# Modulation as matrix products with one moving column, D transform's matrices in eight loads, and a new order in the first stage

## The chip, the cores and the metric

One core of a Trainium2 chip runs the kernel. The metric is the device time of one execution in microseconds. Engines are named as in the profile: PE is TensorE, DVE is VectorE, ACT is ScalarE, POOL is GpSimd, SP is SyncE (which here only issues DMA transfers). Clocks are shares of full speed.

## The reference

`S` is 2048 rows, `D` is 512 columns, `F` is 1792. All data are float32.

```python
mod = (_silu(c) @ w_mod).reshape(c.shape[0], 6, 1, -1)
sa, ca, ga, sb, cb, gb = (mod[:, 0], mod[:, 1], mod[:, 2], mod[:, 3], mod[:, 4], mod[:, 5])
h = _layernorm(x, axis=-1) * (1 + ca) + sa
a = einsum("bsd,ed->bse", h, dft_hid_re)
b = einsum("bsd,ed->bse", h, dft_hid_im)
x = x + ga * (einsum("ts,bse->bte", dft_seq_re, a) - einsum("ts,bse->bte", dft_seq_im, b))
h = _layernorm(x, axis=-1) * (1 + cb) + sb
x = x + gb * ((_silu(h @ w1) * (h @ w3)) @ w2)
```

## The kernel before

The kernel has three stages. The first is the transform along D: eight steps `k`, each of two blocks of 128 rows (a block and its mirror), are loaded, normalised, turned by TensorE, modulated with `sa` and `1 + ca`, split into a high part (float32r, by ScalarE) and a low part (by VectorE), and multiplied with the D transform's matrices. The second stage is the transform along S, the third the gated feed-forward block. Stage two begins with the products at L750.

What the first stage needs ahead of any product is loaded in this order, mostly from SP's queue: the condition `cc`, the first rows `x` (k = 0), four tiles `wm[v, k]` of the modulation's weights (`v` 1 is the scale `ca`, 0 is the shift `sa`; two tiles from ACT's queue, the fourth tile in two loads), the D transform's matrices for two of four column groups `dt` (`raw_w[0]`, `raw_w[1]`: real and imaginary part, 512 KB a tile), the rows of k = 1, the matrices' other two tiles, and the rows of k = 2 and 3. A load's completion is counted on one of eight semaphores in turn, and a load waits for the one eight before it.

A matrix tile has its 128 partitions as two halves `q` of 64: partition 64 q + r holds the source's row (r, q), and in the source q lies inside r. Before, each half of each part is a load of its own, whose source has 64 rows: `queue.dma_start(raw_w[dt][q * 64 : (q + 1) * 64, m, :], w[i][par::2, q])`, 16 loads in all (L231). ScalarE (`w_highs`) and VectorE (`w_lows`, `differ_w`) then make the operands `wu`, `wn` and `wd` of them.

The modulation before: `mod_scale` multiplies the four quarters of a weight matrix by `silu(c)` and adds them up, one ScalarE and three VectorE instructions for each `v`; `mod_sum` sums over the partitions with four 128-column products with ones; `mod_read` copies the sums to `mod1`.

`keep_warm` is a product on data of no use, which keeps TensorE busy while it has nothing to do.

The work of the first stage is put in order by a list scheduler written in the kernel (`task` and `arrange`): each task has a rank (a number from the table `RANK`, plus the step `k` times `PACE`), needs, and a planned duration on an engine; among the tasks that could begin soon the one with the lowest rank is taken. `at` gives the planned times at which loads land and the modulation is there, `clear` the planned times at which the engines are free. These numbers set the order alone; on the chip every engine takes its instructions in that order and waits by semaphores. Where TensorE would stand idle in the plan, while the first products are not there, `arrange` puts in small filler products.

Of the kernel before, what the change touches and what calls it, by code (L numbers as in the profile page):

```python
# [12 lines left out]
OP = mybir.AluOpType  # L13
AX = mybir.AxisListType

P = 128
# [6 lines left out]
ND = D // P  # L23
# [19 lines left out]
def folded(nc, pools, c, cp, wmr, wmc, x, xt, ctr, cti, wdr, wdi, w1, w3, w2, out):  # L43
# [15 lines left out]
    def take(dt=F32, what="s"):  # L59
        slot = free.popleft()  # L60
        count[0] += 1
        t = big.tile([P, 2, N], dt, name=f"{what}_{count[0]}", tag=f"slot{slot}")
        slot_of[id(t)] = (slot, t)
        return t

    def give(t):
        slot, _ = slot_of.pop(id(t))
        free.append(slot)

    def bank(i):  # L70
        count[0] += 1
        return psum.tile([P, N], F32, name=f"bank{i}_{count[0]}", tag=f"bank{i}")

    def flat(t):
        return t.rearrange("p a b -> p (a b)")
# [7 lines left out]
    def cols(i):  # L83
        return slice(i * P, (i + 1) * P)

    def copy(dst, src, scale=1.0):
        nc.scalar.activation(dst, src, AF.Copy, scale=scale)  # L87
# [62 lines left out]
    mirror = consts.tile([P, NT, 2, NK // 2], I32, name="mirror")  # L150
# [64 lines left out]
    wm = {}  # L215
# [8 lines left out]
    raw_w = {}  # L224

    def load_hid(dt, queue):
        i, par = HD[dt]
        raw_w[dt] = take(F32, "w")
        for m, w in enumerate((wdr, wdi)):
            for q in range(2):  # L230
                queue.dma_start(raw_w[dt][q * 64 : (q + 1) * 64, m, :], w[i][par::2, q])  # L231

    nc.sync.dma_start(cc, cp)
    load_x(0, nc.scalar)
# [4 lines left out]
    for dt in range(2):  # L239
        load_hid(dt, nc.sync)  # L240
    load_x(1)
    for dt in range(2, ND):
        load_hid(dt, nc.sync)
# [27 lines left out]
    zero = take(F32, "zero")  # L271
    nc.gpsimd.memset(flat(zero), 0.0)
    first_tmp = take(F32, "tmp")
    onesf = first_tmp[:, 0, :]
# [3 lines left out]
    def keep_warm(count, width=N):  # L278

        for _ in range(count):  # L280
            nc.tensor.matmul(
                warm[:, :width], onesf[:, :P], onesf[:, :width], start=True, stop=True
            )

    sc = consts.tile([P, ND], F32, name="sc")
# [8 lines left out]
    def hid_cols(t, dt):  # L294

        i, par = HD[dt]
        return t[:, 2 * P * i + par : 2 * P * (i + 1) : 2]

    mod_acc = [bank(5), bank(6)]

    def mod_scale(v, h):

        w, own = wm[v, 0][:, 0, :], wm[v, h]
        if h == 0:
            copy_by(w, w, sc[:, 0:1])
        for n in range(1 - h, 2):
            nc.vector.scalar_tensor_tensor(
                w, own[:, n, :], sc[:, 2 * h + n : 2 * h + n + 1], w, op0=OP.mult, op1=OP.add
            )

    def mod_sum(v):

        for dt in range(ND):
            nc.tensor.matmul(
                mod_acc[v][:, cols(dt)],
                hid_cols(wm[v, 0][:, 0, :], dt),
                onesf[:, :P],
                start=True,
                stop=True,
            )  # L320

    def mod_read(v):
        for at in (slice(0, ND),) if v else [slice(dt, dt + 1) for dt in range(ND)]:
            nc.vector.tensor_scalar(
                mod1[:, v, at],
                mod_acc[v][:, ::P][:, at],
                float(v),
                None,
                op0=OP.add,
            )  # L330
        for h in range(2):
            give(wm.pop((v, h)))

    def copy_by(dst, src, by):
        nc.scalar.activation(dst, src, AF.Identity, scale=by)  # L335
# [116 lines left out]
    def norm_root(k):  # L452
        mv, r = rs[k]
        nc.scalar.activation(r[:, 0, :], mv[:, :, 1], AF.Sqrt, bias=eps, scale=1.0)

    def norm_inverse(k):

        mv, r = rs[k]
        nc.vector.reciprocal(r[:, 0, :], r[:, 0, :])
        nc.vector.scalar_tensor_tensor(  # L460
            r[:, 1, :], mv[:, :, 0], -1.0, r[:, 0, :], op0=OP.mult, op1=OP.mult
        )

    def norm_scale(k, side, engine):
        r = rs[k][1]
        a, by, add = xz[k][:, side, :], r[:, 0, side : side + 1], r[:, 1, side : side + 1]
        if engine == "ACT":
            nc.scalar.activation(a, a, AF.Identity, bias=add, scale=by)
        else:
            nc.vector.tensor_scalar(a, a, by, add, op0=OP.mult, op1=OP.add)  # L470


    turned, hm, hs, h1 = {}, {}, {}, {}
    hh, hl = {}, {}
# [5 lines left out]
    def turn_rows(k, side):  # L480
        if side == 0:
            turned[k] = [bank(2 * (k % 2) + h) for h in range(2)]
        for dt in range(ND):
            at = (dt % 2) * HALF + side * P
            nc.tensor.transpose(
                turned[k][dt // 2][:, at : at + P],
                hid_cols(xz[k][:, side, :], dt),
                anti if side and where(k)[1] else ident,
            )
        if side:  # L490
            give(xz.pop(k))
            rs.pop(k)

    def modulate_rows(k, dt, engine):
        if k not in hm:
            hm[k] = take(F32, "hm")
        src = turned[k][dt // 2][:, (dt % 2) * HALF : (dt % 2 + 1) * HALF]
        dst = four(hm[k])[:, dt, :]
        sa, ca1 = mod1[:, 0, dt : dt + 1], mod1[:, 1, dt : dt + 1]
        if engine == "ACT":  # L500
            nc.scalar.activation(dst, src, AF.Identity, bias=sa, scale=ca1)
        else:
            nc.vector.tensor_scalar(dst, src, ca1, sa, op0=OP.mult, op1=OP.add)
# [35 lines left out]
    uh, us, ul = {}, {}, {}  # L539
# [6 lines left out]
    def hid_begin(k):  # L546

        hb[k] = bank(4 + k % 2)
        nc.tensor.matmul(
            hb[k], nought, flat(wt[0] if k else zz)[:, :N], start=True, stop=False, skip_group_check=True  # L550
        )
# [102 lines left out]
    def clear_z():  # L654
        copy(flat(zz), flat(zero))
        give(zero)
# [139 lines left out]
    xr = {}  # L796

    def load_xt(t):
        xr[t] = [take(F32, "xr") for _ in range(2)]
        for i in range(2):  # L800
            nc.sync.dma_start(xr[t][i], xt[t, i])

    def residual(t, e, src, gate):
        xs = xr[t][e // 2][:, e % 2, :]
# [261 lines left out]
    turn = [0, 0]  # L1066
# [360 lines left out]
    clear = {"PE": 0.0, "DVE": 0.0, "ACT": 0.0, "POOL": 0.0, "SP": 0.0}  # L1427
# [32 lines left out]
    def at(us, *names):  # L1460
        for name in names:
            ends[name] = (us, "DMA")

    def last_steps(k):
# [6 lines left out]

    PACE = 7.39
    RANK = {
        "stats": -18.2,
        "root": -47.5,
        "inverse": -47.1,
        "scale": -41.6,
        "turn": -4.3,
        "mod": -3.8,
        "sum": -42.2,  # L1480
        "hh": -19.0,
        "hl": -6.5,
        "h1": -11.0,
        "prod": 2.1,
        "odd": -9.0,
        "mirror": 61.7,
        "uh": 12.4,
        "us": 4.0,
        "ul": 3.9,
        "diff": 21.3,  # L1490
        "up": -6.8,
        "ush": 27.9,
        "ulh": 31.5,
    }
    seq_steps = []
    keep_warm(3)
# [1 line left out]
        norm_stats(0, side)  # L1498
    norm_root(0)
    norm_inverse(0)  # L1500
    for side in range(2):
        norm_scale(0, side, "ACT" if side else "DVE")
        turn_rows(0, side)
    keep_warm(1)
    for v, h in ((1, 0), (1, 1), (0, 0)):
        mod_scale(v, h)
    mod_sum(1)
    copy(nought, zero[:, 0, :P])
    clear_z()
    hid_begin(0)  # L1510
    keep_warm(6, P)
    mod_scale(0, 1)
    mod_read(1)
    mod_sum(0)
    mod_read(0)


    at(10.0, "turn0.0", "turn0.1")
    for dt in range(ND):
        at(13.6 + 0.25 * dt, f"modc{dt}")  # L1520
        at((13.4, 15.2, 18.3, 20.3)[dt], f"w{dt}")
    for k in range(1, 4):
        at((16.5, 21.8, 23.3)[k - 1], f"x{k}")
    clear.update(PE=14.2, DVE=14.5, ACT=12.2, POOL=9.0, SP=9.0)
    for k in range(4, NK):
        task(f"load{k}", 2 * k - 7, [f"wd{min(k - 4, 2) + 1}"], lambda k=k: load_x(k), POOL=1.0)
        task(f"x{k}", 0, [f"load{k}"], lambda: None, **{f"DMA{k}": 6.0})
# [9 lines left out]
    for k in range(NK):  # L1537
        r = k * PACE
        both = [f"{k}.0", f"{k}.1"]
        if k:  # L1540
# [10 lines left out]
            for s in range(2):  # L1551
                task(
                    f"scale{k}.{s}", r + RANK["scale"] + s, [f"inverse{k}"],
                    lambda e, k=k, s=s: norm_scale(k, s, e), ACT=0.71, DVE=0.46,
# [5 lines left out]
        for dt in range(ND):  # L1560
            task(
                f"mod{k}.{dt}", r + RANK["mod"] + 0.1 * dt, [f"modc{dt}", *[f"turn{n}" for n in both]],
                lambda e, k=k, dt=dt: modulate_rows(k, dt, e), ACT=0.45, DVE=0.46,
# [83 lines left out]
    for n, (j, k) in enumerate(steps):  # L1647
        if k == 2:
            load_xt(j + 2)
        if k == 5:  # L1650
            load_xt(j)
# [884 lines left out]
def fnet_swiglu_block(  # L2536
# [26 lines left out]
    pools = consts, small, big, psum  # L2563
    args = c, cp, wmr, wmc, x, xt, ctr, cti, wdr, wdi, w1, w3, w2, out
    bad = folded(nc, (*pools, dram, tc), *args)
    flag = nc.values_load(
        bad[0:1, 0:1],
# [62 lines left out]
```

## Time and profile before

| | us |
|---|---|
| median of 3 runs | 692.43 (691.5 to 692.43) |
| profiled execution, its time | 691.3 |
| its span (first to last instruction) | 689.5 |
| PE busy in the span | 673.1 |
| first product of the D transform (L559) | 21.87 |
| first product of stage two (L750) | 83.76 |

Times in the timelines are counted from the span's start. "idle before <-X" says what ended an engine's wait. A row of a DMA queue has the packets, the megabytes and the time that they took as a share of 16 DMA engines. PE's clock was 0.997 of full speed over the span.

### The profile page before, as it was taken

How to read it: one execution, taken by the hardware profiler on the slowest of the kernel's cores; microseconds unless marked ns; L12 is line 12 of the kernel's file. 1: busy time of each engine (PE TensorE's matmuls, PEld its weight loads, DVE VectorE, ACT ScalarE, POOL GpSimd, SP SyncE). 2: the span in 40 equal slices, each digit the busy share in tenths (PEclk: the TensorE clock that was granted, in tenths of full speed). 3: DMA queues.
4: the chain of work that ended last, by engine and by line, in shares of the span. 5: the costliest groups of instructions: out<-in, count | busy, mean ns of one | idle time of the engine just before them, and what ended most of it. 6: DMA issues, size and time to landing. Idle time of an engine off the chain costs nothing.

```text
span 689.5 us, 9030 instructions
## 1 busy us (share of the span) xinstructions
PE 673.1 (98%) x3122; PEld 557.5 (81%) x3122; DVE 586.7 (85%) x945; ACT 451.2 (65%) x751; POOL 134.2 (19%) x156
## 2 busy tenths in 40 slices
PE   6999999999999999999999999999999999999996
PEld 4898788888888888888788888887878888888785
DVE  5999769997999977989997989787998979888375
ACT  4998956455343665663577767867677887877520
POOL 1320172544435000100101101011012112221100
PEclk9999999999999999999999999999999999999998
DMA  8730199887678441274757666466939998999813
GB/s 264 222 125 1 52 371 329 261 293 262 190 291 291 153 149 30 51 135 122 134 140 127 150 153 123 96 131 120 277 74 213 162 202 165 180 217 170 182 42 126
DMA packets 40262, 116.80 MB, mean 169 GB/s; under 512 B 5137, under 2 KB 5393, under 8 KB 40209
## 3 DMA queue, kind: packets, MB, share of 16 engines
q0 software_dynamic: 14512, 50.86, 36.8%
q1 hardware_dynamic: 25264, 63.98, 27.9%
q10 hardware_dynamic: 432, 1.31, 0.5%
q8 instruction: 26, 0.43, 0.3%
q14 instruction: 28, 0.22, 0.1%
HBM read 76.81 MB, written 41.42 MB: 171 GB/s over the span
## 4 chain that ended last, share of the span: by engine, by line
PE 75%; issue 8%; DVE 7%; ACT 4%; DMA 4%; POOL 1%; SPq 1%; POOLq 0%; DVEq 0%; ACTq 0%
PE bank L100 45%; PE bank L750 26%; DMA sum<-y 2%; PE bank L559 2%; POOL sum L1352 1%; PE bank L598 1%; DMA w<-in_wdr 1%; SPq L231 1%; DVE xr L805 1%; PE bank L576 1%; DMA x<-in_x 1%; ACT y L335 0%; DVE ul L90 0%; DVE hl L90 0%; ACT hh L87 0%
## 5 line engine op out<-in xcount | busy, mean ns | idle before, releaser
L100 PE MATMUL bank<-hf,w2h 128*128 128x512 f32 (+1 forms) x352 | 108.3, 389 | 0.0
L87 ACT ACTIVATE hf<-v 128x512 fp32r<-128x512 f32 x71 | 44.4, 631 | 67.3 <-DVE v L96 54.4
L335 ACT ACTIVATE y<-bank,gb 128x512 f32<-128x512 f32 x118 | 76.5, 682 | 4.0 <-PE bank L100 3.9
L100 PEld LDWEIGHTS bank<-hf,w2h 128*128 128x128 f32 x352 | 65.6, 188 | 15.3 <-ACT y L335 1.5
L1160 POOL DMA_DIRECT2D sum<-y x28 | 24.0, 857 | 240.7 <-ACT y L335 124.6
L100 PE MATMUL bank<-hf,w2l 128*128 128x512 f32 (+1 forms) x176 | 68.2, 387 | 0.0
L90 DVE TENSOR_TENSOR hf<-v,hf 128x512 fp32r<-128x512 f32 x71 | 48.7, 686 | 10.4 <-ACT hf L87 10.3
L1352 POOL DMA_DIRECT2D sum<-y x35 | 29.8, 852 | 128.8 <-ACT y L335 119.8
L87 ACT ACTIVATE x<-bank 128x512 f32<-128x512 f32 x72 | 41.8, 591 | 13.5 <-PE bank L100 12.6
L750 PE MATMUL bank<-l,us 128*128 128x512 f32 x128 | 49.9, 390 | 0.0
L750 PE MATMUL bank<-d,us 128*128 128x512 f32 x128 | 49.9, 390 | 0.0
L750 PE MATMUL bank<-bh,us 128*128 128x512 f32 x128 | 49.9, 390 | 0.0
L750 PE MATMUL bank<-d,uh 128*128 128x512 f32 x128 | 49.9, 390 | 0.0
L750 PE MATMUL bank<-bh,ul 128*128 128x512 f32 x128 | 49.8, 389 | 0.0
L750 PE MATMUL bank<-l,uh 128*128 128x512 f32 x128 | 49.8, 389 | 0.0
L170 POOL DMA_INDIRECT re<-in_ctr,mirror x32 | 36.3, 1136 | 65.5 <-ACT im L188 40.1
L170 POOL DMA_INDIRECT im<-in_cti,mirror x32 | 34.2, 1069 | 32.5 <-PE bank L750 8.5
L93 DVE TENSOR_TENSOR x<-bank,x 128x512 f32<-128x512 f32 x36 | 24.7, 685 | 17.8 <-PE bank L100 17.8
L100 PEld LDWEIGHTS bank<-hf,w2l 128*128 128x128 f32 x176 | 33.1, 188 | 6.7
L1244 ACT ACTIVATE v<-v 128x512 f32<-128x512 f32 x36 | 22.6, 629 | 23.2 <-DVE v L93 22.8
L93 DVE TENSOR_TENSOR v<-bank,x 128x512 f32<-128x512 f32 x36 | 24.7, 686 | 14.9 <-PE bank L100 14.0
L100 PE MATMUL bank<-h2h,w1h 128*128 128x512 f32 x80 | 31.2, 390 | 0.0
(260 smaller groups left out, 1902.1 us busy)
## 6 DMA issues: line engine op xcount, KB each, us to landing
sum<-y POOLq DMA_DIRECT2D x63, 512.0 KB, 5.5
w<-in_w SPq DMA_DIRECT2D x42, 512.0 KB, 5.0
re<-in_ctr SPq DMA_DIRECT2D x32, 256.0 KB, 5.4
im<-in_cti SPq DMA_DIRECT2D x32, 256.0 KB, 5.2
wmc<-in_wmc SPq DMA_DIRECT2D x8, 512.0 KB, 7.9
xr<-in_xt SPq DMA_DIRECT2D x8, 512.0 KB, 8.0
sum<-xr SPq DMA_DIRECT2D x8, 512.0 KB, 6.3
x<-in_x SPq DMA_DIRECT2D x11, 256.0 KB, 4.6
```

What stands on the lines that cost most here:

```text
L87: nc.scalar.activation(dst, src, AF.Copy, scale=scale)
L90: nc.vector.tensor_tensor(out=dst, in0=a, in1=b, op=OP.subtract)
L93: nc.vector.tensor_tensor(out=dst, in0=a, in1=b, op=OP.add)
L100: nc.tensor.matmul(acc, lhs[a], rhs[b], start=first and n == 0, stop=last and n == len(PASSES) - 1, skip_group_check=more,)
L170: nc.gpsimd.indirect_dma_start(dst, None, rows, bass.IndirectOffsetOnAxis(ap=at, axis=0))
L231: queue.dma_start(raw_w[dt][q * 64 : (q + 1) * 64, m, :], w[i][par::2, q])
L335: nc.scalar.activation(dst, src, AF.Identity, scale=by)
L559: nc.tensor.matmul(halves(hb[k])[:, m, :], sides((hh, hl)[a][k])[:, dt, m, :], wu[dt][:, b, m, :], start=False, stop=dt % 2 == 1 and n == ...
L750: nc.tensor.matmul(acc[what, e], lhs, rhs, start=begin and i == 0, stop=(end or (turn and what == "x")) and i == len(terms) - 1, skip_grou ...
L1160: nc.gpsimd.dma_start(sums[t, d // 2], y, accum_op=OP.add)
L1244: behind(k != 0 or q == 0, lambda: nc.scalar.activation(v, src, AF.Silu))
L1352: nc.gpsimd.dma_start(sums[t, which], y, accum_op=OP.add)
```

## The change

Four edits, all but one in the first stage.

The matrices' halves are loaded together: the source is rearranged so that `q` is its outermost dimension, and one load fills 128 partitions; 16 loads become 8. The modulation's weights are used as they land: for each half `h` and each `n`, four products with the weights as the stationary operand and one column of `silu(c)` as the moving one add into four columns of a bank, after a product with zeros has cleared them; the scaling on ScalarE and VectorE goes. The parts stand between the filler, the first turns and `hid_begin(0)`. The table of ranks, the planned times of arrival and the planned free times are new. And the first tile of `xt` that a residual uses is loaded in two halves.

```diff
-            for q in range(2):
-                queue.dma_start(raw_w[dt][q * 64 : (q + 1) * 64, m, :], w[i][par::2, q])
+            queue.dma_start(raw_w[dt][:, m, :], w[i][par::2].rearrange("r q n -> q r n"))
...
-    def mod_scale(v, h):
-
-        w, own = wm[v, 0][:, 0, :], wm[v, h]
-        if h == 0:
-            copy_by(w, w, sc[:, 0:1])
-        for n in range(1 - h, 2):
-            nc.vector.scalar_tensor_tensor(
-                w, own[:, n, :], sc[:, 2 * h + n : 2 * h + n + 1], w, op0=OP.mult, op1=OP.add
-            )
-
-    def mod_sum(v):
-
-        for dt in range(ND):
-            nc.tensor.matmul(
-                mod_acc[v][:, cols(dt)],
-                hid_cols(wm[v, 0][:, 0, :], dt),
-                onesf[:, :P],
-                start=True,
-                stop=True,
-            )
+    def mod_part(v, h):
+        if h == 0:
+            nc.tensor.matmul(
+                mod_acc[v][:, :ND], zero[:, 0, :P], onesf[:, :ND], start=True, stop=False, skip_group_check=True
+            )
+        for n in range(2):
+            for dt in range(ND):
+                nc.tensor.matmul(
+                    mod_acc[v][:, dt : dt + 1],
+                    hid_cols(wm[v, h][:, n, :], dt),
+                    sc[:, 2 * h + n : 2 * h + n + 1],
+                    start=False,
+                    stop=h == n == 1,
+                    skip_group_check=True,
+                )
...
-        for i in range(2):
-            nc.sync.dma_start(xr[t][i], xt[t, i])
+        for q in range(2):
+            nc.sync.dma_start(xr[t][0][:, q, :], xt[t, 0, :, q])
+        nc.sync.dma_start(xr[t][1], xt[t, 1])
...
-        "h1": -11.0,
-        "prod": 2.1,
+        "h1": -67.5,
+        "prod": 22.3,
...
+    mod_part(1, 0)
     for side in range(2):
         norm_scale(0, side, "ACT" if side else "DVE")
         turn_rows(0, side)
-    keep_warm(1)
-    for v, h in ((1, 0), (1, 1), (0, 0)):
-        mod_scale(v, h)
-    mod_sum(1)
+    mod_part(1, 1)
+    mod_part(0, 0)
     copy(nought, zero[:, 0, :P])
     clear_z()
+    mod_part(0, 1)
+    mod_read(1)
+    mod_read(0)
     hid_begin(0)
-    keep_warm(6, P)
-    mod_scale(0, 1)
-    mod_read(1)
-    mod_sum(0)
-    mod_read(0)
...
-        at(13.6 + 0.25 * dt, f"modc{dt}")
-        at((13.4, 15.2, 18.3, 20.3)[dt], f"w{dt}")
+        at(12.9 + 0.1 * dt, f"modc{dt}")
+        at((12.9, 14.5, 17.8, 19.4)[dt], f"w{dt}")
```

The order that follows at the places in question stands in the prediction.

More of the change, by code (lines that the diff above doesn't have):

```diff
@@ L325, in mod_read @@
                 mod1[:, v, at],
-                mod_acc[v][:, ::P][:, at],
+                mod_acc[v][:, at],
                 float(v),
@@ L1473, in folded @@
     RANK = {
[L1474 to L1482, printed above, removed]
-        "h1": -11.0,
-        "prod": 2.1,
[L1485 to L1493, printed above, removed]
+        "stats": -18.3,
+        "root": -6.1,
+        "inverse": -60.4,
+        "scale": -51.2,
+        "turn": -52.0,
+        "mod": -2.1,
+        "sum": -41.7,
+        "hh": 4.4,
+        "hl": -39.1,
+        "h1": -67.5,
+        "prod": 22.3,
+        "odd": 7.5,
+        "mirror": 66.4,
+        "uh": 29.1,
+        "us": 22.3,
+        "ul": 4.1,
+        "diff": 41.9,
+        "up": 8.8,
+        "ush": 56.6,
+        "ulh": 43.1,
     }
@@ L1503, in folded @@
         turn_rows(0, side)
-    keep_warm(1)
-    for v, h in ((1, 0), (1, 1), (0, 0)):
-        mod_scale(v, h)
-    mod_sum(1)
+    mod_part(1, 1)
+    mod_part(0, 0)
     copy(nought, zero[:, 0, :P])
     clear_z()
+    mod_part(0, 1)
+    mod_read(1)
+    mod_read(0)
     hid_begin(0)
-    keep_warm(6, P)
-    mod_scale(0, 1)
-    mod_read(1)
-    mod_sum(0)
-    mod_read(0)
     at(10.0, "turn0.0", "turn0.1")
     for dt in range(ND):
-        at(13.6 + 0.25 * dt, f"modc{dt}")
-        at((13.4, 15.2, 18.3, 20.3)[dt], f"w{dt}")
+        at(12.9 + 0.1 * dt, f"modc{dt}")
+        at((12.9, 14.5, 17.8, 19.4)[dt], f"w{dt}")
     for k in range(1, 4):
-        at((16.5, 21.8, 23.3)[k - 1], f"x{k}")
-    clear.update(PE=14.2, DVE=14.5, ACT=12.2, POOL=9.0, SP=9.0)
+        at((16.1, 21.0, 22.7)[k - 1], f"x{k}")
+    clear.update(PE=13.2, DVE=13.2, ACT=12.0, POOL=9.0, SP=9.0)
     for k in range(4, NK):
```

## The prediction

> **What bounds the kernel now.** I read the page first, then busy time by windows, then the timelines of the first 90 us engine by engine, and then the DMA view in narrow windows, because the change touches only the first stage (apart from four extra loads of `xt`).
>
> ```profile
> span 689.5 us, 9030 instructions
> PE 673.1 (98%) x3122; PEld 557.5 (81%) x3122; DVE 586.7 (85%) x945; ACT 451.2 (65%) x751; POOL 134.2 (19%) x156
> ```
>
> TensorE is busy nearly all the time, so what can move the end is where TensorE idles, or spins on filler. Two windows show where that can be (columns: window, its length, busy us of PE, PEld, DVE, ACT, POOL, granted clock, DMA share, GB/s).
>
> ```profile
> 22.00:84.00 62.00, 59.24 (x397) 53.52 (x398) 58.01 (x113) 57.98 (x119) 11.82 (x14) 1.00 0.28 86
> 83.70:689.50 605.80, 598.14 (x2633) 492.01 (x2632) 515.00 (x795) 380.42 (x611) 119.69 (x127) 1.00 0.69 175
> ```
>
> From 22 to 84 us (the D transform of sixteen row blocks) TensorE, VectorE and ScalarE are all within 4 us of full, so this stretch has a length of its own: TensorE needs 59.2 us of it. After 84 us the second stage starts, and nothing in the change alters its work. The first 22 us are the rest. There TensorE does this:
>
> ```profile
> 2.59 4.56 PE L281 MATMUL bank<-tmp 128*128 128x512 f32 x6 [2.59 <-DVE tmp L275]
> 10.01 1.02 PE L281 MATMUL bank<-tmp 128*128 128x512 f32 x2
> 12.13 1.21 PE L314 MATMUL bank<-tmp,wmr 128*128 128x128 f32 x8 [1.09 <-DVE wmr L307]
> 14.74 1.10 PE L314 MATMUL bank<-tmp,wmr 128*128 128x128 f32 x8
> 15.69 5.75 PE L281 MATMUL bank<-tmp 128*128 128x128 f32 x50
> 21.87 0.51 PE L559 MATMUL bank<-wu,hh 128*128 128x256 f32 x2 [0.44 <-ACT hh L87]
> 83.76 0.39 PE L750 MATMUL bank<-bh,us 128*128 128x512 f32 x1
> ```
>
> L281 is filler. The first real product (L559) stands at 21.87, the second stage (L750) starts at 83.76. What TensorE waits for there is the chain of loads: the chain of waits goes through them until 20.6.
>
> ```profile
> 0.75 3.47 DMA x<-in_x
> 4.24 7.91 DMA w<-in_wdr
> ...
> 17.94 2.67 DMA w<-in_wdi
> 20.60 0.70 ACT wu L87 x2
> ```
>
> The matrices of the D transform (`w`, four tiles of 512 KB) are split by ScalarE as they land; the fourth tile's two pieces go last:
>
> ```profile
> 13.74 0.42 ACT L87 ACTIVATE wu<-w 128x256 fp32r<-128x256 f32 x1 [0.57 <-DMA w<-in_wdi]
> 22.43 0.71 ACT L87 ACTIVATE wu<-w 128x256 fp32r<-128x256 f32 x2
> ```
>
> So the second piece of the fourth tile starts at about 22.43 + 0.35 = 22.78, and 83.76 - 22.78 = 61.0 us of the stage lie behind it.
>
> **The eight loads.** This is the part that decides. On SP's queue, before (the names end in the tile's number, the brackets hold the semaphores waited for):
>
> ```order
> L220 DMA wmr_96<-in_wmr 128x512 x2
> L231 DMA w_99<-in_wdr 64x512 [waits DMAHW0_49]
> L231 DMA w_99<-in_wdr 64x512 [waits DMAHW1_49]
> L231 DMA w_99<-in_wdi 64x512 [waits DMAHW2_49]
> L231 DMA w_99<-in_wdi 64x512 [waits DMAHW3_49]
> L231 DMA w_104<-in_wdr 64x512 [waits DMAHW4_49]
> L231 DMA w_104<-in_wdr 64x512 [waits DMAHW5_49]
> L231 DMA w_104<-in_wdi 64x512 [waits DMAHW6_49]
> L231 DMA w_104<-in_wdi 64x512 [waits DMAHW7_49]
> L209 DMA x_109<-in_x 128x1x512 [waits DMAHW0_49]
> L211 DMA x_109<-in_x 128x1x512 [waits DMAHW1_49]
> ```
>
> and now, on the same queue:
>
> ```order
> L220 DMA wmr_96<-in_wmr 128x512 x2
> L230 DMA w_99<-in_wdr 128x1x512 [waits DMAHW0_49]
> L230 DMA w_99<-in_wdi 128x1x512 [waits DMAHW1_49]
> L230 DMA w_102<-in_wdr 128x1x512 [waits DMAHW2_49]
> L230 DMA w_102<-in_wdi 128x1x512 [waits DMAHW3_49]
> L209 DMA x_105<-in_x 128x1x512 [waits DMAHW4_49]
> L211 DMA x_105<-in_x 128x1x512 [waits DMAHW5_49]
> L230 DMA w_108<-in_wdr 128x1x512 [waits DMAHW6_49]
> L230 DMA w_108<-in_wdi 128x1x512 [waits DMAHW7_49]
> L230 DMA w_111<-in_wdr 128x1x512 [waits DMAHW0_49]
> L230 DMA w_111<-in_wdi 128x1x512 [waits DMAHW1_49]
> ```
>
> Each load waits for the eighth one before it, so halving the count lets SP run ahead: `x_105` no longer waits for `w`, and eight issues go.
>
> ```profile
> 12.17 0.59 SPq L209 DMA_DIRECT2D x<-in_x  x1
> 17.30 1.23 SPq L231 DMA_DIRECT2D w<-in_wdi  x2
> ```
>
> Eight issues of about 0.62 us are 5 us of queue time. That would be worth something only if issue were the limit, and if the eight loads are moved as fast as the sixteen. The second is what I doubt. The source is now counted as 2 (q), 64 (r), 512 (n): its outermost count is 2, where every load of `x`, `wmr` and `w` in this trace has 64 or 128 there. How a load is cut over the 16 DMA engines the packet counts show: up to 12 us the queue of ScalarE (q10) carries three loads of 128 rows.
>
> ```profile
> q10 hardware_dynamic: 432, 1.31, 30.4%
> wmr<-in_wmr ACTq DMA_DIRECT2D x2, 512.0 KB, 6.8
> x<-in_x ACTq DMA_DIRECT2D x1, 256.0 KB, 3.5
> ```
>
> 432 packets are 3 x 128 rows and 3 x 16 more, one completion for each engine: each of these loads was shared out over 16 engines, and all of them have an outer count that 16 divides. If a load is shared out along its outermost count, a source with 2 there gives two shares: two engines move 64 rows each, and fourteen move nothing. In the Trainium skill, DMA: Bandwidth & Descriptors, section Why a DMA increments its semaphore by 16 and not by 1, this is the rule: the number of engines is the largest up to 16 that divides the slowest count of both sides, and loads issued from SP take the lowest-numbered ones; by it these loads go to engines 0 and 1, all eight of them. The same page, section Rules for kernel authors, says of halves of the partitions to use one 128-partition transfer, which speaks for the change; by that alone the first rival below holds. For outer counts of 64 and 128 the packet counts agree with the first rule; no run here shows a small outer count.
>
> What two engines cost. The pace of one engine is bytes over engine time (queue rows: packets, MB, share of 16 engines in a window of 2 us; windows 8 to 10, 10 to 12, 22 to 24):
>
> ```profile
> q1 hardware_dynamic: 292, 0.55, 70.8%
> q1 hardware_dynamic: 311, 0.51, 109.1%
> q1 hardware_dynamic: 236, 0.43, 71.0%
> 5.00:10.00 5.00, 3.18 (x12) 1.58 (x11) 2.76 (x8) 2.23 (x5) 0.00 (x0) 1.00 1.03 408
> 10.00:12.00 2.00, 1.04 (x4) 0.21 (x2) 1.93 (x4) 1.77 (x3) 0.00 (x0) 1.00 1.09 256
> ```
>
> 0.55 MB / (0.708 x 32 us) = 24.3 GB/s; the others 14.6 and 18.9; with larger rows at 5 to 10 us 408/16 = 25.5. The slow rows are those of many 128 KB loads with four rows and a completion for each engine; the new loads have 64 rows for each, so I take 24.3. The four tiles are 2.10 MB, 1.05 MB for each of two engines: 43.2 us (41.2 at 25.5, 55.5 at 18.9, 71.8 at 14.6), 5.4 us a load. The first of today's pieces lands at 4.24 + 7.91 = 12.15 and took 0.131 MB / 256 GB/s = 0.5 us, so the queue in front of `w` is through at about 11.6. Between the second and third tile stand the two loads of `x_105`, 0.033 MB on each engine, 1.3 us. The last piece of `w` then lands at 11.6 + 43.2 + 1.3 = 56.1. The issues do not delay this: the fourth tile's two wait for the first tile's, which are in by 11.6 + 2 x 5.4 = 22.4.
>
> Who waits for it. On ScalarE, around the fourth tile (`w_117` before, `w_111` now; `hh`, `h`, `hm` are the row blocks' operands). Before:
>
> ```order
> L87 ACTIVATE wu_250<-w_112 128x256 x2
> L87 ACTIVATE hh_255<-hs_246 128x4x128
> L468 ACTIVATE x_109<-x_109,rs_235 128x512
> L87 ACTIVATE wu_294<-w_117 128x256 x2
> L87 ACTIVATE hh_255<-hs_246 128x4x128
> L87 ACTIVATE h_35_308<-hm_219 128x512
> L501 ACTIVATE hm_314<-bank_31_288,mod_147 128x256 x2
> ```
>
> Now:
>
> ```order
> L87 ACTIVATE wu_251<-w_108 128x256 x2
> L448 ACTIVATE rs_239<-mv_238,eps 128x2
> L87 ACTIVATE hh_256<-hs_249 128x4x128
> L87 ACTIVATE h_31_258<-hm_222 128x512
> L462 ACTIVATE x_105<-x_105,rs_239 128x512
> L87 ACTIVATE wu_308<-w_111 128x256 x2
> L87 ACTIVATE hh_256<-hs_249 128x4x128
> L495 ACTIVATE hm_317<-bank_32_294,mod_139 128x256 x2
> ```
>
> The place is nearly the same: one `h` went ahead of the fourth tile, and all that follows is queued behind it, the other half of the first block's `hh` and every later block. So ScalarE stands until 56.1, and VectorE and TensorE with it. The shift at this place is 56.1 - 22.78 = 33.3 us, and the 61.0 us behind it are still to come. The loads of `x` for the next blocks lie behind the fourth tile on the same two engines, 0.7 us a load; they land soon after and are no later against it than now.
>
> **The new list.** What it can give back are TensorE's stalls behind that point:
>
> ```profile
> PE bank L549 <- DVE ho L93: 1.8, 2, 1.6
> PE bank L598 <- ACT h L87: 1.0, 1, 1.0
> ```
>
> At most 2.8 us, at least 0 (with VectorE and ScalarE at 58.0 of 62 another order can also lose as much). I take half, -1.4. On the other side TensorE is idle for some 30 us ahead of it, since the list plans 27 fillers and no more. At the start, six filler matmuls took 4.56 us (0.76 each), later two took 1.02 (0.51): after a pause about 4.6 us of work may run at two thirds, +1.5 at most; I take +0.8.
>
> **The modulation.** Six VectorE instructions of 0.75 us and two of ScalarE of 0.71 us go:
>
> ```profile
> L307 DVE SCALAR_TENSOR_TENSOR wmr<-wmr,sc,wmr x4: 752/752/752, 10.5 to 13.6; 128x512 f32<-128x512 f32 x4
> L335 ACT ACTIVATE wmr<-wmr,sc x2: 707/714/722, 9.0 to 9.9; 128x512 f32<-128x512 f32 x2
> 15.89 0.35 DVE L324 TENSOR_SCALAR mod<-bank 128x1 f32<-128x1 f32 x4 [1.50 <-PE bank L314]
> ```
>
> TensorE gets 34 small matmuls, two passes each. Four of today's modulation matmuls take 1.10 to 1.21 us, 0.28 to 0.30 each; with one moving column the weight loads remain, and I take 0.24, a bound from the filler (5.75 us / 25 = 0.23). The parts stand in a row on TensorE behind the warm-up (7.15) and around the transposes (1.2 us), and end at about 7.2 + 34 x 0.24 + 1.2 = 16.5, against today's read at 15.89. With the first tile of `w` landing at 22.4 this is covered: 0. Without that cover it costs 0.6.
>
> **The split load of `xt`** adds four issues of 0.6 us to SP, long before the tile is read; 0, or 0.6 if one stood in front of a load that is waited for.
>
> **Sum.** +33.3 - 1.4 + 0.8 = +32.7. The profiled run took 691.3 us (span 689.5 and 1.8 around it), so 724.0 on its scale; the median of the runs is 692.43, 1.1 above it. I forecast 692.4 + 32.7 = 725.
>
> **The rivals.** (1) The loads go over 16 engines after all, and the list wins its stalls: -2.8, and the modulation's +0.6, is 692.4 - 2.2 = 690.2. For it: 0.62 us of issue for each load, which falls away. Against it: at 10 to 12 us the DMA engines are full (share 1.09) with the queue well ahead, so fewer issues alone bring little. It decides if a `w` load shows 16 completions. (2) Over 16 engines with no stall won: +0.6 from the later modulation, 693.0. (3) Two engines, but another pair for each load: the loads run side by side, the first lands at 11.6 + 5.4 = 17.0, the fourth tile is issued then (its wait) and lands 5.4 to 7 us later, at 22.4 to 24; with the first tile's split 3 us later than 13.74 the start slips by 1 to 2.5 us: 694.2. (4) Inside the forecast, a slower pace: 18.9 GB/s for each engine gives 55.5 instead of 43.2, 737; 14.6 gives 754.
>
> **How the numbers follow.** Two engines, the same pair: 0.86. Rival 1: 0.07; rival 2: 0.03; rival 3: 0.04. The weight of the first is a judgement: every load seen has 16 completions where its outer count has 16 shares to give, and nothing in the trace shows a load shared out along an inner count, which the rivals 1 and 2 need. Its low end is the 25.5 GB/s pace with all stalls won and no slow start, 692.4 + (54.1 - 22.8 - 2.8) = 721; I go to 717 since the stretch behind may close up a little more; its high end is 18.9 GB/s with a slow start, 692.4 + (68.4 - 22.8 + 1.5) = 739.5, and to 742 for the list. That leaves out the rivals 1 to 3 (0.14) and a little of the slow pace. About 0.2% is what a measurement of this kernel can tell from no change (1.4 us): faster by more is rival 1, 0.07; within is rival 2, 0.03; slower is the rest, 0.90.
>
> **What would show it.** In the changed kernel's profile: 130 packets instead of 144 for a `w` load (two completions instead of 16), a `w` load landing some 5 us after the one before it, DMA share near 2/16 from about 12 to 55 us; ScalarE idle before each `wu` on `w`, the last one starting at about 56; second stage at about 116. I am wrong if the fourth tile lands before 30 us; then rivals 1 to 3 are told apart by the completions and by TensorE's first real product (21.87 now).

## The result, and the profile after

| | before | after |
|---|---|---|
| median, 5 runs of each | 692.43 (691.5 to 693.07) | 726.95 (726.43 to 728.2) |
| ratio, 95% interval | | 1.0497 [1.0483, 1.0511] |
| profiled execution, its span | 691.3, 689.5 | 728.2, 726.4 |
| fourth tile's second piece starts on ACT | 22.78 | 55.68 |
| first product of stage two | 83.76 | 118.51 |

The change makes the kernel 34.5 us slower. The page after, first the row of engine busy time, then the granted clock in 40 slices of 18 us:

```profile
span 726.4 us, 9096 instructions
PE 689.3 (95%) x3164; PEld 573.1 (79%) x3164; DVE 584.7 (80%) x943; ACT 449.4 (62%) x745; POOL 132.5 (18%) x156
PEclk7658999999999999999999999999999999999999
```

VectorE and ScalarE do about the work they did (2 us less each), in a longer span. TensorE shows 16 us more than before. The first four slices have a clock of 0.5 to 0.8: by an estimate from the windows, some 25 us of work ran at half clock, which is 12 us of the 16. The rest is mostly the modulation, now 68 products where there were 16.

The timeline of ScalarE has the eight splits of the new loads, each behind idle time that a landing `w` ends (in the brackets); the first and the last two:

```profile
15.92 0.42 ACT L87 ACTIVATE wu<-w 128x256 fp32r<-128x256 f32 x1 [5.54 <-DMA w<-in_wdr]
21.20 0.42 ACT L87 ACTIVATE wu<-w 128x256 fp32r<-128x256 f32 x1 [4.86 <-DMA w<-in_wdi]
...
49.86 0.42 ACT L87 ACTIVATE wu<-w 128x256 fp32r<-128x256 f32 x1 [3.55 <-DMA w<-in_wdr]
55.68 0.42 ACT L87 ACTIVATE wu<-w 128x256 fp32r<-128x256 f32 x1 [5.40 <-DMA w<-in_wdi]
```

The DMA view of 17 to 22 us, SP's queue: packets, MB and share of 16 engines. Two of the 16 would be 12.5%.

```profile
q1 hardware_dynamic: 122, 0.25, 13.0%
```

From 28 to 36 us the share is 13.2%. Loads on several pairs of engines side by side (the third rival) would have shown a multiple of it.

SP's own timeline, the issues:

```profile
4.53 0.62 SPq L230 DMA_DIRECT2D w<-in_wdr  x1
5.20 1.94 SPq L230 DMA_DIRECT2D w<-in_wdi  x1
7.18 4.97 SPq L230 DMA_DIRECT2D w<-in_wdr  x1
...
15.88 7.27 SPq L209 DMA_DIRECT2D x<-in_x  x1
...
35.11 5.15 SPq L230 DMA_DIRECT2D w<-in_wdi  x1
```

The first issue took 0.6 us, as before. From the third on most take 3.6 to 5.4 us, near the 5.3 us that the two engines need for a load: SP stands in the issue itself, and the rows of `x` behind it in its queue are issued late as well.

TensorE's timeline; the bracket has its idle time:

```profile
7.40 2.02 PE L307 MATMUL bank<-sc,wmr 128*128 128x1 f32 x16
...
14.47 6.96 PE L307 MATMUL bank<-sc,wmr 128*128 128x1 f32 x32
...
45.14 1.22 PE L553 MATMUL bank<-wu,hh 128*128 128x256 f32 x4 [14.97 <-ACT hh L87]
...
56.67 1.22 PE L553 MATMUL bank<-wu,hh 128*128 128x256 f32 x4 [7.75 <-ACT hh L87]
...
118.51 0.39 PE L744 MATMUL bank<-bh,us 128*128 128x512 f32 x1
```

The waits of 15.0 and 7.8 us are for ScalarE's `hh`, which is queued behind the splits. And by windows (window, its length, then busy time of PE, PEld, DVE, ACT, POOL, granted clock, DMA share, GB/s) there is something that the prediction did not have:

```profile
9.00:10.00 1.00, 1.00 (x9) 1.00 (x9) 0.00 (x0) 1.00 (x3) 0.00 (x0) 0.84 1.03 397
16.00:20.00 4.00, 4.00 (x20) 4.00 (x21) 0.00 (x0) 0.34 (x1) 0.00 (x0) 0.50 0.14 53
28.00:30.00 2.00, 2.00 (x20) 1.98 (x18) 0.00 (x0) 0.00 (x0) 0.00 (x0) 1.00 0.13 50
46.00:60.00 14.00, 6.25 (x25) 5.57 (x25) 4.99 (x13) 3.48 (x8) 1.29 (x2) 0.50 0.57 177
```

From 10 to 21 us TensorE is busy all the time, nearly all of it with the modulation's products of one column, and the granted clock is 0.50: a pass takes 0.2175 us (6.96 / 32) where it took 0.126 (2.02 / 16). The clock is full again some 5 us into the 128-column filler that follows. After the idle stretch it is 0.50 once more, until about 61 us.

What follows from the start of stage two on, which the prediction took to be unaltered, is 2.1 us longer than before in this execution (726.4 - 118.51 = 607.9 us against 689.5 - 83.76 = 605.7). Nearly all of it is one wait of its products for a tile `xr` of the residual:

```profile
PE bank L744 <- DVE xr L800: 2.0, 1, 2.0
```

### The profile page after: what moved, and what is told of

It is laid out like the page before. It is cut to its first block, busy times and chain, and to the rows that moved or that the text cites. A ratio compares the mean times of both kernels' runs of the same rounds, so it can differ in the third digit from the quotient of the medians.

```text
span 726.4 us, 9096 instructions
## 1 busy us (share of the span) xinstructions
PE 689.3 (95%) x3164; PEld 573.1 (79%) x3164; DVE 584.7 (80%) x943; ACT 449.4 (62%) x745; POOL 132.5 (18%) x156
## 3 DMA queue, kind: packets, MB, share of 16 engines
q1 hardware_dynamic: 25600, 63.98, 26.3%
## 4 chain that ended last, share of the span: by engine, by line
PE 77%; DVE 10%; DMA 4%; SPq 4%; ACT 2%; issue 2%; DVEq 0%; ACTq 0%
PE bank L100 52%; PE bank L744 21%; SPq L230 3%; DMA w<-in_wdi 3%; PE bank L592 1%; PE bank L553 1%; SPq L209 1%; DVE d L93 1%; DMA wmc<-in_wmc 1%; DVE hl L90 1%; DVE xr L800 1%; DVE l L90 1%; DMA x<-in_x 1%; DVE st L443 0%; PE bank L479 0%
## 5 line engine op out<-in xcount | busy, mean ns | idle before, releaser
L87 ACT ACTIVATE x<-bank 128x512 f32<-128x512 f32 x72 | 41.9, 592 | 14.6 <-PE bank L100 12.5
L553 PE MATMUL bank<-wu,hh 128*128 128x256 f32 x128 | 24.9, 295 | 23.9 <-ACT hh L87 22.7
L553 PEld LDWEIGHTS bank<-wu,hh 128*128 128x128 f32 x128 | 20.9, 198 | 25.8 <-ACT hh L87 23.2
```

The lines of the kernel that those rows point to most:

```text
L553: nc.tensor.matmul(halves(hb[k])[:, m, :], sides((hh, hl)[a][k])[:, dt, m, :], wu[dt][:, b, m, :], start=False, stop=dt % 2 == 1 and n == ...
```

## The experiments

Two theories stood after the result. A: two DMA engines carry nearly the whole loss, and with the old loads back only the slow modulation is left, less what the list returns (694 to 698). D: the width of the loads, or the earlier issue, hurts, whatever the number of engines. The half clock was a third question.

**The sixteen loads back, all else changed.**

```diff
-            queue.dma_start(raw_w[dt][:, m, :], w[i][par::2].rearrange("r q n -> q r n"))
+            for q in range(2):
+                queue.dma_start(raw_w[dt][q * 64 : (q + 1) * 64, m, :], w[i][par::2, q])
```

> The changed kernel with the sixteen loads of before; modulation, list and the split load of xt stay. Theory A (the loads' outer count of 2 costs nearly all of the 34.5 us): the fourth tile's last split starts near 22 to 28 us instead of 55.68, the loads' cost is gone. What is left is the modulation on TensorE at the half clock seen in the changed kernel (read at 21.48 instead of 15.89): the first product comes 4 to 6 us later than 21.87, the list takes back 0 to 2.8 us, 694 to 698 us. Rival B (the modulation costs no more than the predicted 0.6 us once the loads are right): 690 to 693. Rival C (modulation and list hold a large part of the 34.5 us themselves): over 705.

Measured: 702.53 (701.42 to 703.76), 1.0141 [1.0123, 1.016] of a kernel before at 693.16. The loads' 24 us are gone, but the rest of the change costs 9.4 us by itself. That is more than A left for it, and less than rival C asks for. TensorE's timeline in this run:

```profile
16.06 6.97 PE L308 MATMUL bank<-sc,wmr 128*128 128x1 f32 x32
23.46 7.93 PE L281 MATMUL bank<-tmp 128*128 128x128 f32 x52
31.14 0.73 PE L554 MATMUL bank<-wu,hh 128*128 128x256 f32 x4
```

and VectorE's read of the modulation:

```profile
23.06 0.35 DVE L319 TENSOR_SCALAR mod<-bank 128x1 f32<-128x1 f32 x4 [7.09 <-PE bank L308]
```

The modulation is read at 23.06 where it was 15.89, and the filler behind it takes 7.93 us instead of 5.75. The first D product comes at 31.14 instead of 21.87. In this execution the first rows of `x` also landed later: VectorE begins with them at 7.52 and not at 5.82. In the profiled executions shown here this time lies between 5.72 and 7.52, and no cause is shown.

**The eight loads alone on the kernel before.**

```diff
-            for q in range(2):
-                queue.dma_start(raw_w[dt][q * 64 : (q + 1) * 64, m, :], w[i][par::2, q])
+            queue.dma_start(raw_w[dt][:, m, :], w[i][par::2].rearrange("r q n -> q r n"))
```

> The kernel before with the eight loads as the only edit; modulation, list and ranks of before. Theory A: the fourth tile's last split starts near 55.7 us and the time is 724 to 729 us. Rival C (a large part of the loss is the modulation's or the list's): 705 to 718.

Measured: 728.34 (727.7 to 729.93), 1.0512 [1.0494, 1.053]. The loads alone make the whole loss. Fourth tile's last split and start of stage two:

```profile
55.51 0.42 ACT L87 ACTIVATE wu<-w 128x256 fp32r<-128x256 f32 x1 [5.18 <-DMA w<-in_wdi]
118.03 0.39 PE L749 MATMUL bank<-bh,us 128*128 128x512 f32 x1
```

So behind these loads the modulation and the list cost nothing that can be measured: the intervals of this run and of the change overlap. Behind the last split lie 62.5 us here, with the old list, against 61.0 before. That 1.5 is the slow clock at the restart: the first product behind the split comes 0.98 us after it here and 0.93 before, the products of `wn` and `h` 4.35 and 2.80 us after it, the granted clock between them is 0.50 here and 1.00 before, and the difference stays 1.5 to the end of the stage.

**Eight loads with 64 outermost.** The changed kernel without the rearrangement of the source; rows then land on other partitions, and the products combine other columns, with the same shapes and amounts.

```diff
-            queue.dma_start(raw_w[dt][:, m, :], w[i][par::2].rearrange("r q n -> q r n"))
+            queue.dma_start(raw_w[dt][:, m, :], w[i][par::2])
```

> The changed kernel, its eight loads kept, the same rows from the same addresses, but with the source's 64 outermost (r, q, n) instead of 2 (q, r, n). The matrices' rows land on other partitions than the turned blocks' columns, so the products combine other columns. Theory A: 144 packets for each load, the fourth tile in by 20 to 22 us, time within 1.5 us of the same kernel with sixteen loads (693 to 698 us). Rival D (eight large loads are slow as such, by their size, their destination or their number in flight): about 727 us.

Measured: 700.45 (700.37 to 701.35), 1.011 [1.0093, 1.0127]. The same count of loads and bytes without the loss: D is refuted. The time is above the 693 to 698 that were expected. SP's queue at 12 to 16 us, here and (second row) in the kernel before:

```profile
q1 hardware_dynamic: 849, 1.55, 105.2%
```

```profile
q1 hardware_dynamic: 635, 1.09, 104.9%
```

Both fill the 16 engines, and the 128-row loads move 1.42 times the bytes in it. The remaining 7.3 us look like those of the first run: the modulation is read at 21.3, and the clock is half. The run with 128 moving columns below tests that.

**Four engines, and eight.** The kernel before, sixteen loads, with the source's 64 rows counted 4 x 16 and 8 x 8 (rows permuted within a half, so the products combine other columns; the diff shows the 4):

```diff
-                queue.dma_start(raw_w[dt][q * 64 : (q + 1) * 64, m, :], w[i][par::2, q])
+                queue.dma_start(raw_w[dt][q * 64 : (q + 1) * 64, m, :], w[i][par::2, q].rearrange("(b a) n -> a b n", a=4))
```

> The kernel before, with its sixteen loads of 64 rows, each with its source counted as 4, 16, 512 instead of 64, 512 (the same rows; they land on other partitions, so the products combine other columns). Theory A (as many DMA engines as the outer count): 80 packets for each load... 64 rows and 4 completions, each engine 16 rows, 16 x 84 ns = 1.34 us for a load, 21.5 us for sixteen; the last one lands at 11.6 + 21.5 + 1.3 = 34.4 us instead of about 22, the time is 701 to 707 us. Rival D: as before, 692 us.

> The kernel before with its sixteen loads of w, each source counted 8, 8, 512 instead of 64, 512 (rows land on other partitions, so the products combine other columns). Theory: eight engines at 24.3 GB/s each move the 2.10 MB in 10.8 us and x between them in 0.3, so the fourth tile lands at about 11.6 + 11.1 = 22.7, some 2 us after today's, where the run with 4 showed 36.2: the time is 692.5 to 696. Rival, the cost is not in the number of engines but in cutting the rows of one load out of order: about as with 4, over 702.

Measured: 707.31 (706.48 to 707.75), 1.0203 [1.0186, 1.022] with 4, and 696.54 (695.25 to 700.75), 1.0051 [1.0029, 1.0073] with 8. SP's queue at 16 to 20 us, with 4 and with 8:

```profile
q1 hardware_dynamic: 246, 0.46, 32.3%
```

```profile
q1 hardware_dynamic: 420, 0.76, 52.8%
```

The last splits of the fourth tile:

```profile
36.19 0.42 ACT L87 ACTIVATE wu<-w 128x256 fp32r<-128x256 f32 x1 [2.56 <-DMA w<-in_wdi]
```

```profile
25.44 0.42 ACT L87 ACTIVATE wu<-w 128x256 fp32r<-128x256 f32 x1 [0.71 <-DMA w<-in_wdi]
```

With 2, 4 and 8 in the outermost place the share is 13.0, 32.3 and 52.8% (2, 4 and 8 of 16 are 12.5, 25 and 50). At the start of its window the run with 4 still has rows of `x` to move, which go over all 16; from 17 to 20 us its share is 26.0%. The last split starts at 55.5, 36.2 and 25.4 instead of 22.78, and the time is 35, 14 and 3 us above before. Both times are just above the expected range (707 and 696).

The 3 us of the run with 8 are not the loads' alone. In its profiled execution the first rows of `x` came 1.3 us later and the modulation was read at 17.78 instead of 15.89; ScalarE waits 3.3 us for it, and only 0.7 for `w` at the last split.

The packets say more exactly how many engines took part. SP's queue over the whole execution, in the kernel before, with the eight loads alone, with 4 and with 8:

```profile
q1 hardware_dynamic: 25264, 63.98, 27.9%
q1 hardware_dynamic: 25024, 63.98, 25.8%
q1 hardware_dynamic: 25072, 63.98, 26.6%
q1 hardware_dynamic: 25136, 63.98, 27.1%
```

The bytes are the same, and the loads of `w` are all that differs. Counted as in the prediction's 432 packets, a load of 64 rows over 16 engines has 64 + 16 = 80, one for each row and a completion for each engine, and the sixteen loads have 1280. The eight then have 240 fewer, 1040, which is 130 for each: 128 rows and 2 completions, the sign that the prediction named. With 4 it is 192 fewer, 68 a load, with 8 it is 128 fewer, 72 a load: 64 rows and 4 or 8 completions. (The expectation's 80 for the run with 4 was a slip.) The changed kernel has 25600 packets and the same with 64 outermost 25712, which is 14 more for each of the eight loads: 144 and 16 completions instead of 130 and 2.

**Wide loads in the right order, without and with the list.** The host lays the two matrices once more as `wdf[i, par, m]`, 128 rows of 512, in the order of the partitions. Modulation as before; the second run adds the new ranks and planned times.

```diff
...
-        for m, w in enumerate((wdr, wdi)):
-            for q in range(2):
-                queue.dma_start(raw_w[dt][q * 64 : (q + 1) * 64, m, :], w[i][par::2, q])
+        for m in range(2):
+            queue.dma_start(raw_w[dt][:, m, :], wdf[i, par, m])
...
```

> The kernel before with eight loads whose source is counted 128, 512: the host lays the two matrices once more in the order of the tiles' rows (a further input), and one 256 KB load fills all 128 partitions of one matrix of a tile. Modulation and list are those of before; the same products are computed. Theory: the number of the outermost count is what hurt, and the loads' count and width are harmless: 16 engines move each load, at the 390 GB/s that the run with 64 outermost showed, so that the fourth tile lands at about 18 us where it landed at about 20.5. The first D product at 21.87 waits for the row block's own chain (hh), not for w, so the gain is small: 690.5 to 693.5. Rival, the loads of w still bind the start, as the chain of waits names them: the 2.5 us come through whole, about 690. Rival, wide loads delay the loads of x behind them: 694 or more.

> As the run with relaid loads, with the changed kernel's list (ranks and planned landing times) on top, the modulation still that of before. Against that run only the list differs. Theory: the list takes about half of TensorE's 2.8 us of stalls between 22 and 84 us: 1 to 2 us faster than the relaid loads alone, 689 to 692. Rival, the list fits only the changed kernel's timing and costs: 1 to 3 us slower, 693 to 696.

Measured: 695.14 (694.44 to 698.28), 1.0023 [1.0009, 1.0037], and with the list 696.5 (693.81 to 701.11), 1.0047 [1.0024, 1.0071], of a kernel before at 693.5 on this chip. The expected gains (690.5 to 693.5, and 689 to 692) did not come. Loads at 388 GB/s instead of 273 in the same window (12 to 16 us) bring nothing. ScalarE, first run:

```profile
12.10 0.84 ACT L87 ACTIVATE wu<-w 128x256 fp32r<-128x256 f32 x2
15.98 1.02 ACT L500 ACTIVATE hm<-bank,mod 128x256 f32<-128x256 f32 x2 [3.03 <-DVE mod L323]
...
22.32 0.72 ACT L87 ACTIVATE wu<-w 128x256 fp32r<-128x256 f32 x2
```

The first tile is split before the modulation is there, and ScalarE then waits 3.0 us for `mod`, not for `w`. The last load of `w` is issued by 12.9 us instead of 18.5, and still the fourth tile's split starts where it did (22.32, 22.43 before), and so does stage two (83.66, 83.76 before). So `w` does not bound the start of the kernel before. The waits name the modulation in its place. No run makes the modulation earlier, so that is not tested. Those that make it later agree: read at 17.9 instead of 15.9 in the run with 128 moving columns below, the first D product came at 24.22 instead of 21.87; read at 21.3 and 23.1, it came at 28.71 and 31.14, there behind filler that ended later too.

Why the median is 1.6 us above before, when the first stage is as long, is open. The profiled execution is the slowest of its runs (698.28), and all that it has more lies behind the start of stage two; 2.1 us of it are the same wait for `xr`:

```profile
PE bank L749 <- DVE xr L804: 2.1, 1, 2.1
```

The list alone has no effect that these runs can tell: the two intervals overlap. Its waits, TensorE's, in the second run:

```profile
PE bank L484 <- DVE x L469: 2.6, 2, 1.8
...
PE bank L558 <- ACT ho L87: 1.2, 2, 0.9
PE bank L558 <- ACT hh L87: 0.6, 1, 0.6
PE bank L575 <- DVE ul L90: 0.3, 1, 0.3
```

The two stalls of 2.8 us in all that the prediction listed are gone, and behind the first D product 1.2 for ScalarE's `ho`, 0.8 of the 2.6 for `x` and 0.3 for `ul` have come. From the first D product to stage two it is 62.7 us (22.57 to 85.23), TensorE idle for 2.4 of them, against 61.9 without the list (21.78 to 83.66), idle for 2.7. So the list exchanged stalls for others and did not shorten the stretch.

**The modulation with 128 moving columns.** The changed kernel with the relaid loads, and the condition's column repeated. The product with zeros clears the whole bank, and `mod_read` takes every 128th column of it.

```diff
...
-                    mod_acc[v][:, dt : dt + 1],
+                    mod_acc[v][:, cols(dt)],
                     hid_cols(wm[v, h][:, n, :], dt),
-                    sc[:, 2 * h + n : 2 * h + n + 1],
+                    sc[:, 2 * h + n : 2 * h + n + 1].to_broadcast([P, P]),
...
```

> The changed kernel with the relaid loads, and each modulation product with the condition's column repeated 128 times as the moving side (128x128 products into a whole bank, of which every 128th column is read). The same sums; each TensorE instruction takes some 0.15 us instead of 0.126 at full clock. To be compared with the run with 64 outermost, which differs by the one-column products (clock 0.50 from 10 to 27 us, modulation read at 21.3, first D product at 28.7, 700.45 us). Theory: products of one column are too little work to keep the clock up, although TensorE is 100% busy with them; with 128 columns the granted clock stays at 1.0, the modulation is read at about 18.7 and the first D product starts at 24 to 26: 693 to 697. Rival, the clock falls for another reason (the pause before the first product, the loads running beside it): it falls here too, at half clock 64 instructions of 0.3 us are 19 us, and the modulation is read at 27 or later: over 703.

Measured: 695.7 (694.6 to 696.51), 1.0029 [1.0013, 1.0045], where one column gave 1.011. Its TensorE:

```profile
13.94 3.92 PE L307 MATMUL bank<-sc,wmr 128*128 128x128 f32 x32
...
24.22 0.73 PE L553 MATMUL bank<-wu,hh 128*128 128x256 f32 x4 [0.32 <-ACT hh L87]
```

its windows at 10 and 14 us:

```profile
10.00:14.00 4.00, 4.00 (x31) 3.53 (x30) 0.16 (x1) 1.12 (x3) 0.00 (x0) 1.00 1.06 391
14.00:18.00 4.00, 4.00 (x35) 3.96 (x34) 0.10 (x2) 0.00 (x0) 0.00 (x0) 1.00 1.05 386
```

and the same windows with one column and 64 outermost:

```profile
10.00:14.00 4.00, 4.00 (x24) 4.00 (x23) 0.00 (x0) 1.49 (x3) 0.00 (x0) 0.59 1.06 391
14.00:18.00 4.00, 4.00 (x20) 4.00 (x20) 0.16 (x1) 0.00 (x0) 0.00 (x0) 0.50 1.05 387
```

The DMA traffic is the same to 1 GB/s, TensorE is busy 4.00 of 4.00 in both, and the clock is 1.00 with 128 columns, and 0.59 and then 0.50 with one. Products 128 times as wide take 0.1225 us a pass (3.92 / 32) and are faster than the narrow ones at half clock, 0.2175. The first D product comes at 24.22 instead of 28.71. So the narrow products cost 4.8 us of the 7.3 that were left with 64 outermost. The 2 us that stay are near the 1.6 of the relaid loads alone.

None of these versions beats the kernel before.

## Why the prediction was right, and where its steps were not

**The two engines**: right, and shown. The last split was forecast at 56.1 and stands at 55.68; the shift at this place, +33.3, is +32.9. The spacing of the splits has a smallest step of 5.28 against 5.4, and 1.3 more where two loads of `x` stand between, as forecast. A load has 130 packets. The runs with 4, 8 and 64 show that it is the outermost count, not the number of loads. This was the mechanism that was forecast, and not luck.

By the Trainium skill, DMA: Bandwidth & Descriptors, section Why a DMA increments its semaphore by 16 and not by 1, the engines used are the largest number up to 16 that divides the slowest count of both sides. The 2, 4 and 8 completions of a load for counts of 2, 4 and 8 agree. The same page's advice, in Rules for kernel authors, to join two halves of the partitions into one transfer holds here for the pace (1.55 against 1.09 MB in 4 us), though the kernel gained nothing by it (695.14), and fails for this source, whose join puts a 2 outermost.

**SP runs ahead**: false. Most issues of the new loads stand 3.6 to 5.4 us in SP, so `x_105`, which went at 12.17, went at 15.88 and its issue took 7.27. It cost nothing that shows, since the share stood at two engines or more all the time and the last split came no later than forecast.

**The list**, -1.4 of stalls: mis-sized. The stalls went as said and others came. On top of the slow restart the stretch behind the last split is 0.3 us longer with the new list (62.8 = 118.51 - 55.68) than with the old one (62.5), in one profiled execution of each, and with the relaid loads the stretch from the first D product is 0.8 longer.

**The slow TensorE after the pause**, +0.8 (0 to 1.5): the upper end, 1.5. So the sum at stage two reads 32.9 + 0.3 + 1.5 = 34.7, not 32.7, and stage two starts at 118.51, not 116. The medians differ by 34.5; the forecast of 725 is 2 us low by these two terms, less 0.4 at the split.

**Behind the start of stage two**, and the split load of `xt`, put at 0 to 0.6: the profiled execution has 2.1 us more there, with the wait for `xr`, and it is 1.3 us above the median. No run changes the split load alone. The wait also stands in the run with relaid loads (2.1), which loads `xt` as before, and does not in the run with 128 columns, which has the split load; so it is not shown to come from the split.

**The modulation**: 0 under the cover was right, 0.6 without it was too small by some eight times. The end at 16.5 was worked out with full-clock passes, and 34 x 0.24 = 8.2 us holds for a full clock only: the read came at 21.48. Without the cover the whole rest of the change costs 7.3 us (64 outermost) to 9.4 (sixteen loads), and 4.8 of it go with 128 columns. So the rivals 1 and 2, at 690.2 and 693.0, did not describe this change: with 16 engines the runs came out at 700 to 703. The forecast did not depend on it, because the first tile's second piece is split at 21.20 in any case.

In the Trainium skill, TensorE: Matmul & The Clock Gate, Part 1, the clock goes by how busy TensorE has been over windows of about 3.4 us. The times fit that order: it fell between 9 and 10 us, some 2 us after the first of these products, and was back 5 us after wide filler began here, and 2.7 us after it in the run with 64 outermost. But busy in that sense cannot be the busy of the profile, which was 100% here; what it counts instead, these runs do not show.

**The chain**: the prediction read from the chain of waits that the loads of `w` bound the start. The relaid loads show that they do not: they go out sooner and at a higher pace, and nothing moves. It is true of the change only because its loads became 33 us later.

## What to carry to other kernels

Before joining loads, look at the source's outermost count as the transfer will carry it: 2, 4 and 8 there meant 2, 4 and 8 of 16 DMA engines, and this kernel was then 35, 14 and 3 us slower (the 3 not by the loads alone). Where the layout is ours, put 64 or 128 outermost: both kept all 16 busy here. A long row of products with one moving column kept TensorE busy in the profile and let its clock fall to half, for themselves and for what followed, so price them at the half clock, or give them wide moving sides. And test a bound that the chain names by making that thing earlier: here `w` came earlier, and nothing followed.

## What the runs showed of the hardware

- A load whose source had 2, 4 or 8 outermost has the packets of 2, 4 or 8 completions instead of 16 (130, 68 and 72 packets a load), and moved at a DMA share of 13.0, 26.0 and 52.8%.
- One-column products alone: clock 0.50 at 100% busy; 128-column products in their place: 1.00.
- In windows in which the 16 engines were full, loads of 128 rows of 2 KB moved at 385 to 391 GB/s, and with loads of 64 rows in the place of those of `w` it was 256 to 273 GB/s, at a share of 1.05 to 1.10.
- With two engines at work, an issue on SP took up to 5.4 us for a load of `w` and up to 7.3 for rows of `x` behind one, instead of 0.6.
